# A scan and a gated feed-forward layer in fp32: weight exponents moved to ScalarE, norm scales folded into the weights, two gate tiles ahead of the norm, and every block written as a list of small steps

## The chip, the cores and the metric

The kernel runs on one core of one Trainium2 chip. The metric is device time in microseconds (us); the figure shown for a kernel is the median of its runs. The core's engines are TensorE (PE for its matmuls, PEld for its weight loads), VectorE (DVE), ScalarE (ACT), GpSimd (POOL) and SyncE (SP), which here issues nearly all DMAs. Each engine executes its own list of instructions in order, and semaphores make one engine wait for another.

## The reference

A chunked state-space scan over 4 batches x 8 heads x 768 tokens feeds a gated feed-forward layer over 3072 tokens x 256 channels.

```python
for c in range(nc):                       # chunks of 32 tokens
    cum = np.cumsum(la, axis=-1)          # la = log(clip(a))
    L = np.exp(cum[..., :, None] - cum[..., None, :]) * causal
    M = np.einsum('bhin,bhjn->bhij', Cc, Bc) * L
    y_intra = np.einsum('bhij,bhjd->bhid', M, xc)
    y_inter = np.einsum('bhin,bhnd->bhid', Cc, state) * np.exp(cum)[..., None]
    state = decay_full * state + sum(Bx)
x = y.transpose(0, 2, 1, 3).reshape(B * S, H * D)
xn = x / np.sqrt(np.mean(x * x, -1) + 1e-6) * rms_g
g = xn @ w_gate                           # 256 x 1536
out = (g / (1 + np.exp(-g)) * (xn @ w_val)) @ w_out   # 1536 x 256
```

The three weight matrices come in float64; the other inputs are float32.

## The kernel before, in words

The scan works in chunks of 128 tokens, two at a time: a *pair* `p` of 256 tokens. There are 12 pairs. Two pairs make a *block* of 512 tokens, of which there are six (0 to 5), and the feed-forward layer works block by block. While PE runs block `b`'s feed-forward products, the scan of block `b + 1` is threaded between them.

**Weights.** Float64 weights arrive as pairs of 32-bit words in 20 pieces (`fetch`): four small ones of 2 x 128 columns, ten of 2 x 256 for gate and value, six of the output matrix. `begin` and `finish` turn a piece into fp32. DVE masks the exponent bits (L157), ACT turns them into a power of two in two passes (L160, L161), DVE builds the mantissa (L163, L166), ors the sign into the power (L172) and multiplies (L174). At most nine pieces are fetched ahead; the next fetch is issued by a `begin`.

**Scan of a pair.** `pad` spreads C into a zeroed tile (GpSimd, in pair 0 half of it DVE, L384), `scale` multiplies B and C by decays, `turn` transposes them on PE (L405) and copies them out of PSUM (L407), `products` form C times B (L428) and multiply by the decay matrix `L` (L436, L447), `states` form the new state (L459 to L476), `outputs` sum up (L494, L503), square on ACT (L519), add on GpSimd (L520) and copy out (L521). For the first four pairs the decay matrices come from PE (`mask`, `sums`) and an exponential; later ones are broadcast by a DMA from a table in DRAM (`spread`, L367), reduced by a subtraction on DVE (L373), exponentiated (L376) and masked on GpSimd (L377).

**Norm.** `norm_sums` makes the mean square on PE (L531) and the inverse root on GpSimd (L536); `norm_apply` spreads it by a PE transpose (L544) and multiplies on DVE by the norm and by `rms_g` (L550).

**Feed-forward.** In block 0, 12 tiles of gate and value (L567, 128 x 512 each), a silu (L575), a product (L580), then the projection (L688). Blocks 1 to 5 use a seven-product scheme over 2 x 2 blocks of the operands, which replaces one of eight products by additions: for each pair of tiles `j` (six of them) products 1 to 7 (L619) into two PSUM banks, with copies on ACT (L624), sums `c` (L629), silus (L634) and hidden products (L638) between them; then the projection in the same scheme (L724), whose operands are made by in-place differences of the hidden tiles on DVE (L709, L710, L756, L762). `combine_w`, `combine_x`, `combine_wo` make the operands' combinations.

**Order.** The tile framework is told to keep the order of the program text, so each engine's list is the order in which the Python calls stand. In block 0 that is a hand-written sequence with lists of conversions per tile (`plan`) and of scan steps per tile (`scan_steps`); in blocks 1 to 5 it is the loop in `gates_and_values` and the sequence in `projection`, with scan steps hung into it (`todo`, `extras`).

## Time and profile before

| | |
|---|---|
| Time, median of 3 runs | 448.68 us (448.5 to 453.81) |
| The profiled execution, its own time | 445.7 us |
| Its span | 444.0 us |
| PE / DVE / ACT busy | 425.4 / 321.1 / 197.7 us |
| Granted TensorE clock | 1.0 |

A row of a timeline gives the start, the time from the first start to the last end of a run of like instructions, the engine, the line, the operation, output and input tiles, shape and count; the bracket is the engine's idle time ahead of it and who ended it. A matmul of fp32 shows as two records, so x16 are eight matmuls. A row of the grouped views gives, behind the bar, busy time, mean nanoseconds of one, and the idle time ahead with its releaser. Since PE's ends are modelled and overlap the next start, its standing time is better read from starts.

### The profile page before, as it was taken

Reading aid. Unit: us, or ns where it says so; the run is one execution under the profiler, and the core shown is the slowest. Engines: PE = TensorE matmul, PEld = TensorE weight load, DVE = VectorE, ACT = ScalarE, POOL = GpSimd, SP = SyncE. Lnnn points to the kernel's source line nnn. Section 1 sums busy time; section 2 is a strip of 40 time slices with the busy share of each in tenths; the row PEclk is TensorE's granted clock in tenths of the full one; section 3 lists DMA queues with packets and bytes.
Section 4 is the critical chain, followed back from the end, with each engine's and each line's share of the span. In section 5 each row is a group of like instructions: output and inputs, shape, how many; then the busy total and the mean of one; then the engine's idle time right before and its main releaser. Section 6 shows DMA issues by size and latency. Waiting matters only on the chain.

```text
span 444.0 us, 7771 instructions
## 1 busy us (share of the span) xinstructions
PE 425.4 (96%) x3066; PEld 340.6 (77%) x3066; DVE 321.1 (72%) x669; ACT 197.7 (45%) x370; POOL 51.7 (12%) x73
## 2 busy tenths in 40 slices
PE   7988999898999998999998999998999999999996
PEld 4654454386777788987788987788987789988896
DVE  5769997589887988466858566868557855467661
ACT  3467553435644353446453446453345440155510
POOL 4030000013200005100005200004200001000000
PEclk9999999999999999999999999999999999999999
DMA  9884443760433120432320341330100000100001
GB/s 137 182 208 138 153 119 103 228 86 0 83 37 81 38 97 3 73 47 47 73 96 2 67 52 26 94 96 1 48 1 1 0 1 1 47 3 0 1 1 47
DMA packets 86564, 27.99 MB, mean 63 GB/s; under 512 B 76000, under 2 KB 80352, under 8 KB 86528
## 3 DMA queue, kind: packets, MB, share of 16 engines
q1 hardware_dynamic: 82368, 27.24, 26.7%
q10 hardware_dynamic: 4160, 0.26, 0.8%
q8 instruction: 24, 0.39, 0.3%
q14 instruction: 12, 0.10, 0.1%
HBM read 24.22 MB, written 3.28 MB: 62 GB/s over the span
## 4 chain that ended last, share of the span: by engine, by line
PE 82%; DVE 11%; SPq 2%; DMA 2%; issue 1%; ACT 0%; POOL 0%; DVEq 0%
PE gate L619 24%; PE o L724 21%; PE val L619 17%; PE gate L567 6%; PE g L428 4%; PE y L503 3%; PE tp L405 2%; SPq L108 2%; PE y L494 2%; DMA xr<-in_x_dram 1%; DVE e L172 1%; PE o L688 1%; DVE L L373 1%; DVE s L756 1%; DVE m L166 1%; DVE sw L597 1%
## 5 line engine op out<-in xcount | busy, mean ns | idle before, releaser
L629 DVE TENSOR_TENSOR c<-val,p 128x512 f32<-128x512 f32 x90 | 60.7, 687 | 44.6 <-PE val L619 36.8
L624 ACT COPY p<-gate 128x512 f32<-128x512 f32 x90 | 52.8, 587 | 51.9 <-PE gate L619 51.7
L619 PE MATMUL gate<-tx,sw 128*128 128x256 f32 x240 | 63.7, 388 | 0.7 <-ACT p L624 0.7
L634 ACT ACTIVATE c<-c 128x256 f32<-128x256 f32 x90 | 37.8, 420 | 46.4 <-DVE c L629 46.4
L619 PEld LDWEIGHTS gate<-tx,sw 128*128 128x128 f32 x240 | 42.7, 190 | 9.9 <-issue 3.3
L638 DVE TENSOR_TENSOR h<-c 128x256 f32<-128x256 f32 x90 | 37.7, 419 | 12.6 <-ACT c L634 12.6
L567 PE MATMUL gate<-xn,wgv 128*128 128x512 f32 x96 | 43.7, 599 | 1.2 <-DVE wgv L174 1.2
L724 PE MATMUL o<-two,s 128*128 128x128 f32 x240 | 30.4, 278 | 4.1 <-DVE s L756 4.1
L520 POOL TENSOR_TENSOR sq<-sq 128x256 f32<-128x256 f32 x12 | 8.9, 744 | 218.3 <-ACT sq L519 218.3
L567 PEld LDWEIGHTS gate<-xn,wgv 128*128 128x128 f32 x96 | 17.3, 190 | 20.4 <-issue 17.4
L377 POOL TENSOR_SCALAR_AFFINE_SELECT L<-L 128x1024 f32<-128x1024 f32 x16 | 24.7, 1552 | 68.1 <-ACT L L376 68.1
L724 PEld LDWEIGHTS o<-two,s 128*128 128x128 f32 x240 | 28.2, 192 | 5.1 <-ACT v L735 2.4
L619 PE MATMUL val<-xn,sw 128*128 128x256 f32 x120 | 31.7, 386 | 0.0
L619 PE MATMUL val<-tx,sw 128*128 128x256 f32 x120 | 31.3, 383 | 0.1
L619 PE MATMUL gate<-tx,wgv 128*128 128x256 f32 x120 | 30.9, 380 | 0.0
L619 PE MATMUL gate<-xn,wgv 128*128 128x256 f32 x120 | 30.8, 379 | 0.0
L619 PE MATMUL val<-xn,wgv 128*128 128x256 f32 x120 | 30.8, 379 | 0.0
L724 PE MATMUL o<-wo,h 128*128 128x128 f32 x240 | 30.0, 275 | 0.0
L724 PEld LDWEIGHTS o<-wo,h 128*128 128x128 f32 x240 | 29.2, 192 | 0.5
L376 ACT ACTIVATE L<-L 128x1024 f32<-128x1024 f32 x16 | 16.9, 1057 | 28.4 <-DVE L L373 28.1
L724 PE MATMUL o<-two,h 128*128 128x128 f32 x240 | 27.6, 275 | 0.0
L724 PEld LDWEIGHTS o<-two,h 128*128 128x128 f32 x240 | 27.2, 192 | 0.0
(147 smaller groups left out, 706.8 us busy)
## 6 DMA issues: line engine op xcount, KB each, us to landing
L<-rowd SPq DMA_DIRECT2D x16, 512.0 KB, 4.7
xr<-in_x_dram SPq DMA_DIRECT2D x24, 128.0 KB, 3.1
wr<-in_moe_w_out_dram SPq DMA_DIRECT2D x6, 512.0 KB, 3.4
wr<-in_moe_w_gate_dram SPq DMA_DIRECT2D x5, 512.0 KB, 5.9
wr<-in_moe_w_val_dram SPq DMA_DIRECT2D x5, 512.0 KB, 4.9
out_dram<-ob SPq DMA_DIRECT2D x10, 256.0 KB, 2.1
br<-in_B_dram SPq DMA_DIRECT2D x22, 64.0 KB, 2.9
cr<-in_C_dram SPq DMA_DIRECT2D x22, 64.0 KB, 3.0
```

What stands on the lines that cost most here:

```text
L376: nc.scalar.activation(out=L, in_=L, func=AF.Exp)
L377: nc.gpsimd.affine_select(out=L, in_=L, pattern=[[0, NH], [1, P]], compare_op=ALU.is_ge, fill=0.0, base=0, channel_multiplier=-1)
L428: nc.tensor.matmul(out=g[:, 256 * i:256 * i + 256], lhsT=T[r, i, 0], rhs=T[r, i, 1:3].rearrange("p t m -> p (t m)"), start=(i == 0), stop= ...
L503: nc.tensor.matmul(out=y[o:o + 32, h // 4, i * P:(i + 1) * P], lhsT=s["x"][:, i, h], rhs=Ls[p][:, i, h], start=opens, stop=True, tile_posi ...
L520: nc.gpsimd.tensor_tensor(out=sqs[blk][:, tk], in0=sq2[:, 0], in1=sq2[:, 1], op=ALU.add)
L567: nc.tensor.matmul(out=gv[:, k], lhsT=w[:, t, fs], rhs=xns[blk][:, t], start=(t == 0), stop=(t == 1))
L619: nc.tensor.matmul(out=dst[:, half[w]], lhsT=lhsT, rhs=rhs[k], start=(opens and w == 0), stop=True, skip_group_check=True)
L624: nc.scalar.copy(out=t, in_=src)
L629: nc.vector.tensor_tensor(out=c, in0=b, in1=a, op=ALU.add)
L634: nc.scalar.activation(out=u, in_=c[:, half[0]], func=AF.Silu)
L638: nc.vector.tensor_tensor(out=hidden_tile(blk, j)[:, f, k], in0=u, in1=c[:, half[1]], op=ALU.mult)
L724: nc.tensor.matmul(out=o[:, t * P:(t + 1) * P], lhsT=lhsT[:, t], rhs=rhs, start=(opens and j == 0 and t == 0), stop=True, skip_group_check ...
```

## The change

The computation is the same. Five things differ:

- **Powers of two.** ACT reads the top 16 bits of each double (sign, exponent, four bits of mantissa) and makes the signed power of two as a bf16 in three passes: a relu with a 16-bit integer result and two parametric relus. DVE's exponent mask and its sign step are gone; DVE keeps the mantissa (two steps) and the last product, which now issues the next fetch. ACT loads its function table four times more often in all.
- **Norm scales.** `rms_g` times 2^-20 is the scalar of the gate and value weights' last product, which is therefore made in two halves of 128 input channels; the norm's application is one product of 128 x 1024 in place of two of 128 x 512.
- **Two tiles ahead of the norm.** Gate and value tiles 0 and 1 of block 0 are multiplied from the scan's output itself, each in two halves of 256 tokens (`early`); DVE multiplies the result by the inverse root, once for the gate and once for the value (`norm`), and ACT's silu then works in place.
- **Small steps.** Functions are split where one engine hands over to another (`sums_of_logs` and `three_parts`, `turn` and `turned`, `products` and `decayed`, `states`, `outputs`, `norm_sums`, `gates_and_values`, `projection`), and all that follows the set-up is two lists of such steps: one for the head and block 0, one that serves blocks 1 to 5 (a step that has no block to work for is skipped). Block 0's PSUM slots are given out by a small bookkeeping (`take`, `leave`).
- **Engines.** The copies of the scan's output of pairs 0 and 1 move from ACT to DVE.

```diff
+    def power(k):
+        words16, (lo, hi), dst, shape, is_o = fetched[k]
+        n = shape[1] * shape[2]
+        e = cvt.tile([P, n], FP32, tag="e", name="e")
...
+        nc.scalar.activation(out=k16, in_=words16, func=AF.Relu, scale=1.0 / 16, bias=kinks[:, 0:1])
+        nc.scalar.activation(out=g, in_=k16, func=AF.Prelu, scale=-1.0, bias=kinks[:, 1:2],
+                             alpha=2.0 ** -20)
+        nc.scalar.activation(out=b16, in_=g, func=AF.Prelu, scale=-2.0 ** 27, bias=kinks[:, 2:3],
+                             alpha=2.0 ** -20)
...
+    def weight(k):
+        words16, (lo, hi), dst, shape, is_o = fetched[k]
+        e, f = parts.pop((k, "e")), parts.pop((k, "f"))
+        if is_o:
+            nc.vector.scalar_tensor_tensor(out=dst, in0=f, scalar=2.0 ** -20, in1=e,
+                                           op0=ALU.mult, op1=ALU.mult)
+        else:
+            for t in range(2):
+                nc.vector.scalar_tensor_tensor(out=dst[:, t], in0=f[:, t], scalar=g20[:, t:t + 1],
+                                               in1=e[:, t], op0=ALU.mult, op1=ALU.mult)
+        fetch()
...
-    def norm_apply(blk, ks):
...
+    def norm_apply(blk):
+        rb = ps["rb"].rearrange("p k m -> p (k m)")
+        xns[blk] = nrm.tile([P, 2, TB], FP32, tag="xn", name="xn", bufs=1)
+        nc.vector.tensor_tensor(out=xns[blk], in0=yts[blk],
+                                in1=rb.unsqueeze(1).to_broadcast([P, 2, TB]), op=ALU.mult)
...
+    def products_early(f, s, gv):
+        ps["gv", f] = gv
+        fs = slice(f * P, (f + 1) * P)
+        tk = slice(s * 256, s * 256 + 256)
+        for k, w in enumerate((wg, wv)):
+            for t in range(2):
+                nc.tensor.matmul(out=gv[:, k, tk], lhsT=w[:, t, fs], rhs=yts[0][:, t, tk],
+                                 start=(s == 0 and t == 0), stop=(t == 1),
+                                 skip_group_check=True)
...
+    def normed(f):
+        gv = ps.pop(("gv", f))
+        us[f] = ffn.tile([P, TB], FP32, tag="u", name="u", bufs=2)
+        for k, dst in enumerate((us[f], of_block_0(f))):
+            nc.vector.tensor_tensor(out=dst, in0=gv[:, k], in1=ps["r"], op=ALU.mult)
...
+    order = """
+        pad.0 mask.0.1 r.0 d mask.0.0 c parts.0 turn.0.0 dx turn.0.1 T.0.0 cx sums.0.0 pad.1 exp.0.0
...
```

In the list of blocks 1 to 5, `P.k.j` is gate product `k` of tile pair `j`, `O.k.j` the same of the projection, `sub.g` the subtraction for chunk `g` of the block after next, `ms`, `rs`, `rb`, `xn` the norm of the next block. How this moves instructions shows at three places.

**DVE, first weights and the norm of block 0.** `e`, `m` and `wgv` are the exponent, the mantissa and the finished gate and value weights; `me` is the mean square, `yt` the scan's output. Before:

```order
L157 TENSOR_SCALAR e<-wr 128x256
L163 TENSOR_SCALAR m<-wr 128x256
L166 SCALAR_TENSOR_TENSOR m<-wr,m 128x256
L534 TENSOR_SCALAR me<-ms 128x4
L172 SCALAR_TENSOR_TENSOR e<-wr,e 128x256
L174 SCALAR_TENSOR_TENSOR wgv<-m,e 128x2x128
```

Now:

```order
L489 TENSOR_TENSOR L<-g,L 128x2x2x256 x3
L524 TENSOR_TENSOR A<-A_ps,tmask 128x128
L534 SCALAR_TENSOR_TENSOR S<-S,fcol,A 128x64 x2
L190 SCALAR_TENSOR_TENSOR wgv<-m,g_190,e 128x128 x2
L587 COPY yt<-y 128x2x256
```

The first weights are finished right behind the scan of pair 1, ahead of the norm's mean square, and no exponent step of DVE stands among them.

**DVE, projection of block 0.** `wo` are the output weights, `tok` the sums that are subtracted from the broadcast decay tile `L`. Before:

```order
L157 TENSOR_SCALAR e<-wr 128x512
L163 TENSOR_SCALAR m<-wr 128x512
L166 SCALAR_TENSOR_TENSOR m<-wr,m 128x512
L172 SCALAR_TENSOR_TENSOR e<-wr,e 128x512
L174 SCALAR_TENSOR_TENSOR wo<-m,e 128x512
L373 TENSOR_TENSOR L<-L,tok 128x1024
```

Now:

```order
L600 TENSOR_SCALAR me<-ms 128x4
L175 TENSOR_SCALAR m<-wr 128x512
L178 SCALAR_TENSOR_TENSOR m<-wr,m 128x512
L186 SCALAR_TENSOR_TENSOR wo<-m,e 128x512
L408 TENSOR_TENSOR L<-L,tok 128x1024 x3
L186 SCALAR_TENSOR_TENSOR wo<-m,e 128x512
L618 TENSOR_TENSOR xn<-yt,rb 128x1024
```

Three steps make a piece in place of five, and the last pieces are done between the subtractions, before the norm of block 1.

**PE, end of the gate products of blocks 1 to 5.** `ms` and `rb` are the norm's sums and its spread root; `s` and `two` are the combined operands of the projection. Before:

```order
L724 MATMUL o<-two,s 128x128 x2
L531 MATMUL ms<-mean_194,sq 128x1 x4
L724 MATMUL o<-two,s 128x128 x12
L724 MATMUL o<-wo,h 128x128 x12
L544 MATMUL rb<-ident,rs 128x128 x4
```

Now:

```order
L795 MATMUL o<-two,s 128x128 x2
L595 MATMUL ms<-mean_195,sq 128x1 x4
L716 MATMUL val<-xn,sw 128x256 x2
L716 MATMUL gate<-tx,wgv 128x256 x2
L795 MATMUL o<-two,s 128x128 x4
L795 MATMUL o<-wo,h 128x128 x6
L795 MATMUL o<-two,s 128x128 x2
L608 MATMUL rb<-ident,rs 128x128 x4
```

The sums of the norm stand ahead of the last gate products, and groups of the projection's first and fifth product lie between them and the spread root.

More of the change, by code (lines that the diff above doesn't have):

```diff
@@ L800 @@
-    turn(0, 1, nc.vector.tensor_copy, 3)
-    sums([(1, 0, ey)])
-    decay(1, 0, ey)
-    products(0, 0)
-    pad(1, nc.gpsimd)
-    turn(1, 0, nc.scalar.copy, 3)
-    turn(1, 1, nc.scalar.copy, 3)
-    ez = masked()
-    sums([(0, 1, ez)])
-    decay(0, 1, ez)
-    scale(0)
-    products(1, 0)
-    full_ps = bank("full_ps", (P, NC, BH))
-    nc.tensor.matmul(out=full_ps.rearrange("p c h -> p (c h)"), lhsT=ones, rhs=laf,
-                     start=True, stop=True)
-    nc.scalar.activation(out=full, in_=full_ps, func=AF.Exp)
@@ L944 @@
+    """
+    for step in order.split():
+        kind, *numbers = step.split(".")
+        kinds[kind](*map(int, numbers))
     nc.scalar.preload_act_table(AF.Silu)
```

722 lines of the change are left out of this document (340 added, 382 removed).

## The prediction

> **What bounds the kernel now.** I read the page's first and fourth part, then the stretches by stage, then the timeline of TensorE (PE) alone for the places where it stands still. First the page:
>
> ```profile
> PE 425.4 (96%) x3066; PEld 340.6 (77%) x3066; DVE 321.1 (72%) x669; ACT 197.7 (45%) x370; POOL 51.7 (12%) x73
> ...
> PE 82%; DVE 11%; SPq 2%; DMA 2%; issue 1%; ACT 0%; POOL 0%; DVEq 0%
> ```
>
> PE is the bound, and VectorE (DVE) is what it waits for. The stretches run from the last scan output of block 0 to its third gate tile, the other gates of block 0, its projection, block 1, block 3. Columns are the stretch, its length, busy time (instructions) of PE, PEld, DVE, ACT and POOL, granted clock, DMA share, GB/s.
>
> ```profile
> 25.01:40.18 15.17, 13.09 (x84) 6.66 (x81) 11.77 (x29) 13.45 (x21) 3.37 (x6) 1.00 0.58 130
> 40.18:88.69 48.51, 46.23 (x242) 21.85 (x242) 40.95 (x76) 23.73 (x40) 1.45 (x2) 1.00 0.51 158
> 88.69:113.86 25.17, 22.96 (x109) 19.38 (x110) 23.56 (x38) 11.66 (x14) 5.80 (x5) 1.00 0.31 38
> 113.86:181.00 67.14, 64.96 (x498) 54.81 (x497) 58.74 (x124) 30.54 (x63) 10.71 (x11) 1.00 0.25 56
> ...
> 248.00:315.00 67.00, 65.87 (x508) 56.76 (x507) 46.92 (x97) 30.85 (x59) 9.95 (x11) 1.00 0.27 56
> ```
>
> From 40 to 114 us DVE is busy 64.5 of 73.7 us: the weights' conversion is there. In block 3 it has 20 us to spare, and PE is nearly full. The clock is full throughout. So a gain can only be PE's standing time, which I take from starts: what lies between two starts less the dense time of the first group.
>
> ```profile
> 10.99 0.33 PE L405 MATMUL tp<-ident,cp 128*128 128x128 f32 x1 [0.89 <-DVE cp L384]
> ...
> 23.24 0.45 PE L494 MATMUL y<-T,S 32*64 32x128 f32 x8 [0.74 <-ACT T L415]
> ...
> 29.13 0.65 PE L544 MATMUL rb<-ident,rs 128*128 128x128 f32 x4 [0.87 <-POOL rs L536]
> ...
> 31.34 7.19 PE L567 MATMUL gate<-xn,wgv 128*128 128x512 f32 x16
> 38.37 0.27 PE L405 MATMUL tp<-ident,br 128*128 128x128 f32 x1
> ...
> 40.18 3.67 PE L567 MATMUL gate<-xn,wgv 128*128 128x512 f32 x8 [1.21 <-DVE wgv L174]
> ...
> 53.51 1.13 PE L428 MATMUL g<-T 32*128 32x256 f32 x8 [0.87 <-DVE h L580]
> ```
>
> ```profile
> 83.58 3.70 PE L567 MATMUL gate<-xn,wgv 128*128 128x512 f32 x8
> 88.69 1.99 PE L688 MATMUL o<-wo,h 128*128 128x256 f32 x8 [1.41 <-DVE h L580]
> ...
> 101.17 3.72 PE L688 MATMUL o<-wo,h 128*128 128x256 f32 x16 [0.52 <-DVE wo L174]
> 105.93 3.72 PE L688 MATMUL o<-wo,h 128*128 128x256 f32 x16 [1.04 <-DVE wo L174]
> 110.30 3.72 PE L688 MATMUL o<-wo,h 128*128 128x256 f32 x16 [0.65 <-DVE wo L174]
> 113.86 1.03 PE L619 MATMUL gate<-xn,wgv 128*128 128x256 f32 x4
> 114.72 1.03 PE L619 MATMUL val<-xn,wgv 128*128 128x256 f32 x4
> 116.42 1.13 PE L619 MATMUL gate<-tx,sw 128*128 128x256 f32 x4 [0.67 <-ACT p L624]
> ```
>
> Sixteen gate matmuls take 38.37 - 31.34 = 7.03 us, so eight take 3.52: after 83.58 the next could start at 87.10 and starts at 88.69, 1.6 us late. Sixteen of L688 take 113.86 - 110.30 = 3.56, so the steps of 4.76 and 4.37 lose 1.20 and 0.81. A bracket is smaller than such a loss by about 0.2 us, since PE's modelled end overhangs the next start. A gate product of block 1 takes 114.72 - 113.86 = 0.86. Counted so, the places ahead of 40.18 lose 1.1, 0.9, 1.0 and 1.4; those from there to 113.86 lose 1.0, 1.6, 0.7, 1.2 and 0.8. Block 1 opens with 0.8. Within a block there is one place, here in block 3:
>
> ```profile
> 301.55 0.95 PE L531 MATMUL ms<-mean,sq 128*128 128x1 f32 x8
> 303.18 0.68 PE L724 MATMUL o<-two,s 128*128 128x128 f32 x4 [0.68 <-DVE s L756]
> 304.31 1.94 PE L724 MATMUL o<-two,s 128*128 128x128 f32 x15 [0.45 <-DVE s L756]
> ```
>
> PE waits for DVE's in-place differences (L756), 0.9 and then 0.6 us.
>
> **The change part by part.** (a) Conversion. The rows of one 512-column weight piece, among the DVE groups with shapes kept apart, with three that later steps use:
>
> ```profile
> L629 DVE TENSOR_TENSOR c<-val,p 128x512 f32<-128x512 f32 x90 | 60.7, 687 | 44.6 <-PE val L619 36.8 <-ACT p L624 7.5
> L638 DVE TENSOR_TENSOR h<-c 128x256 f32<-128x256 f32 x90 | 37.7, 419 | 12.6 <-ACT c L634 12.6
> ...
> L172 DVE SCALAR_TENSOR_TENSOR e<-wr,e 128x512 int32<-128x512 int32 x16 | 11.9, 744 | 2.1 <-ACT e L161 2.1
> L166 DVE SCALAR_TENSOR_TENSOR m<-wr,m 128x512 f32<-128x512 uint32 x16 | 11.1, 695 | 0.5
> ...
> L580 DVE TENSOR_TENSOR h<-u,gate 128x512 f32<-128x512 f32 x12 | 8.2, 682 | 4.7 <-ACT u L575 4.7
> ...
> L157 DVE TENSOR_SCALAR e<-wr 128x512 int32<-128x512 int32 x16 | 7.0, 439 | 0.1
> L174 DVE SCALAR_TENSOR_TENSOR wgv<-m,e 128x512 f32<-128x512 f32 x10 | 6.9, 692 | 0.3
> L163 DVE TENSOR_SCALAR m<-wr 128x512 int32<-128x512 int32 x16 | 6.7, 422 | 0.0
> ...
> L174 DVE SCALAR_TENSOR_TENSOR wgv<-m,e 128x256 f32<-128x256 f32 x4 | 1.7, 425 | 0.1
> ```
>
> And on ACT:
>
> ```profile
> L624 ACT COPY p<-gate 128x512 f32<-128x512 f32 x90 | 52.8, 587 | 51.9 <-PE gate L619 51.7
> ...
> L161 ACT ACTIVATE e<-e,einf 128x512 int32<-128x512 f32 x16 | 11.6, 722 | 0.5
> ```
>
> DVE loses L157 and L172, 0.44 + 0.74 = 1.18 us a piece, and pays 2 x 0.425 - 0.692 = 0.16 where a gate or value piece is now multiplied in two halves. With 10 such pieces, 6 of the output weights and four small ones at about half, that is 10 x 1.02 + 6 x 1.18 + 4 x 0.5 = 19 us less on DVE, 18 of them between 25 and 114. Given back there are two tiles normed by hand (four 512-wide products like L580's, 0.68 each) and two copies of the scan's output (about 0.6 each, below L580's): 4 us. DVE then has about 62 us of work in the 89 us that were, where 76.3 us are busy now. Of this nothing is gained by itself; it lets DVE be in time.
>
> Scalar (ACT) does three passes in place of two. No row shows the parametric relu or a 16-bit result; nearest is L161, 0.72 us. Below it lies L624's 0.59, also 512 wide; above it twice the row if 16-bit words went at half speed. I take 0.72: a piece costs 2.2 us, 20 pieces add 18 x 0.72 = 13 us (small ones at half), and ACT has 23.73 + 11.66 = 35.4 busy in 73.7 us: covered. At twice the row, 48 large passes add 35 us, more than the cover leaves.
>
> The Trainium skill's "ScalarE: Activation LUTs", section "What ACT_TABLE_LOAD costs", gives 280 ns plus 0.833 ns an element for any function with a bias by pointer; worked out, an estimate of 0.706 us for 512, near the 0.722 row. It says so of fp32 and bf16 alone; by it the rival with dear passes would have no chance at all.
>
> (b) Head, to gate tile 2. The order puts the transposes before the decay sums, both block-0 halves first, and lets two gate tiles run on the un-normed output. The losses of 1.1 (pad copy on DVE, which now comes before the log sums), 0.9 and 1.0 go; PE has the row sums, transposes and pair-2 sums to do meanwhile. For the 1.4 (weights late behind DVE) a new wait comes: the second early tile needs its fourth small piece, whose step on DVE stands behind the root of the norm, two scalings and one mantissa. From the copy of the second output on (24.5) DVE has a mantissa and a weight step of a small piece, four steps of log-sum parts, another mantissa (to about 28.2), waits for PE's `ms` (29.2), then two scalings (0.8), a large mantissa (L163 and L166, 1.1) and the small weight step (0.5): 31.7. PE has two early halves (1.8 each), masks, `ms`, two decay sums and, after GpSimd's root, the turned norm: 31.1. So 4.4 less 1.0 for that and small ones: **3.4**, of which I keep 2.9, since the start still hangs on the loads.
>
> (c) Gates of block 0: 1.0 + 1.6. The `g` products find their bank earlier, and the projection no longer starts behind the last gate: its first group and a scan output stand between gate tile 10 and the next groups. **2.4**.
>
> (d) Projection: 0.7 + 1.2 + 0.8 = 2.7. DVE's work between gate 10 and the last group is 20 us (three weight steps, four subtractions at 1.2, two combinations of four at 0.42, the norm) against 22 us of PE. **2.3**.
>
> (e) Block 1 opens without waiting for ACT's copies, since the four exponentials end before the last group, and its first transposes and products of two tiles lie between: **1.0**.
>
> (f) Norm and differences in blocks 1 to 4: 0.9 + 0.6, in block 4 0.9 alone, 5.4 in all. Two gate products and five output groups now stand between `ms` and the first `6` product. DVE has to do, from the last gate product on, one subtraction (1.22), the last sum `c` (L629, 0.69), six hidden products (L638, 0.42), three sums of the same width: about 5.5 us with what has begun, then 1.3 to the difference of tile 0; PE has seven output products of 0.45 (four records each; 15 take 1.94 with the overhang), the turned norm at 0.5 and six more products before it needs it: 6.4 us. So about 0.4 stays there and 0.4 where the `7` products need DVE again: 0.8 a block, 3 in all. **2.4**.
>
> The sum is 2.9 + 2.4 + 2.3 + 1.0 + 2.4 = 11.0 us; less 0.5 for the two split tiles and the extra switches of tile shape, **10.5**. Table loads rise by four, which ACT's idle 36 us a block hide. The profiled execution took 445.7 us (span 444.0), so 435.2; the median shown is 448.68, so 438.2.
>
> One more row bears on (f): GpSimd's mask of the decays (L377) runs beside DVE.
>
> ```profile
> L373 DVE TENSOR_TENSOR L<-L,tok x16: 1210/1218/2104, 101.0 to 313.9; 128x1024 f32<-128x1024 f32 x16
> ...
> L377 POOL TENSOR_SCALAR_AFFINE_SELECT L<-L x16: 1087/1290/2941, 103.4 to 316.2; 128x1024 f32<-128x1024 f32 x16
> ...
> DMA to landing us min/median/max: 3.4/4.7/7.0
> ```
>
> The third row is the landing time of the broadcasts that fill this tile. A subtraction of 1.22 us takes up to 2.10 then. In the new order two masks fall on the differences; if DVE runs at half speed beside each, it loses 0.6 to a mask, and (f) falls to 2.4 - 3.6 and the time is 441.8. The Trainium skill's "GPSIMD Engine Reference", section "1. Specifications", speaks against the change here: GpSimd shares its SBUF interface with DVE and contends with DVE instructions of two SBUF inputs, which the differences are. That the stretched subtraction has two such inputs agrees with it; that most of the sixteen stand at 1218 ns shows that it does not always bite.
>
> **The rivals.** First, **PE's waits come back elsewhere**: the two engines are packed against each other, and a wait on DVE delays ACT and PE in turn. For it speaks that DVE has by my count 17 us of work in the 20 us of a block's output products, against it its 20 idle us a block. If (f) gives nothing, and half of (c) and (d) returns: 10.5 - 2.4 - 2.4 = 5.7, hence 443 us.
>
> Second, the slower side: **DVE stands for a load in the middle of a block**. The subtraction for the first of the next pairs moved from the projection to between the gate products, and the broadcast that feeds it can only start when the block's first scan output has left the buffer. On the SP queue the next pair's loads stand behind that broadcast, which no one needs within 10 us. Behind the subtraction on DVE stand the sums and hidden products that free the bank for PE's fifth tile. Between that output and the subtraction PE runs five gate products and the `g` products (L428, 1.1): 5 x 0.86 + 1.1, so DVE gets there 5.3 us after that output. At a landing of 4.7 there is no wait, at 7.0 it is 1.8 us in three blocks, 5.4; from 8.7 us on the gain is eaten, and at the 9.2 us that a weight load took in the crowded first 40 us (the row below, of the raw weight tile in that window) it is 3 x 4.0 = 12, hence 450 us.
>
> ```profile
> DMA to landing us min/median/max: 3.6/5.1/9.2
> ```
>
> Against it: DMA share is 0.27 in block 3.
>
> Third, ACT's passes at twice the row: of the 40 us that ACT is idle between 25 and 114, 13 go to the third pass and 7 to the shorter stretch, and 35 us on the 20 that are left cost 15, hence 453 us.
>
> **How the numbers follow.** My forecast 0.55; waits come back 0.35; the load 0.06; dear passes 0.04. Its own range is 433 to 441. The range 431 to 446 takes in 443, contended masks (441.8) and, below, a block phase without any wait (5.4 in place of 2.4, and 1.4 more at the head: 433.8, with 3 us for the scatter of the median). Two per cent, about what a measurement can tell from no change, is 9.0 us: 439.7. The forecast lies 1.5 us inside. Faster: three quarters of the forecast and a third of the first rival, 0.53. Slower by over 2% (457.7): only the far ends of the last two and what I have not seen, 0.04. Within: 0.43.
>
> **What would show it.** DVE's conversion rows fall by about 19 us and ACT's three rows stand at 0.7 us; the first group of block 1 (113.86 now) starts at 106 to 108; no wait of PE for `wo` over 0.3; blocks 2 and 3 take 66.0 to 66.5 in place of 67.0. It is wrong if a PE wait of over 1 us stands in every block, if the 16-bit passes exceed 1 us, or if DVE idles at the mid-block subtraction.

## The result, and the profile after

The changed kernel takes **426.73 us** (median of 4 runs, 425.22 to 426.94), the kernel before 448.59 (448.01 to 453.81) beside it: a ratio of 0.9489, with a 95% interval of 0.9423 to 0.9554. The forecast was 438.2 with a range of 431 to 446: the sign was right, and the gain of 21.9 us was twice the 10.5 foreseen. Executions in which the clock was down for long are left out of the comparisons below; the one of 453.81 is still in here, and without it the ratio is 0.951.

The first and the fourth part of the page of the changed kernel:

```profile
PE 418.5 (98%) x3082; PEld 348.3 (82%) x3082; DVE 305.5 (72%) x645; ACT 209.6 (49%) x393; POOL 50.7 (12%) x73
...
PE 91%; DVE 5%; issue 1%; DMA 1%; POOL 0%; DVEq 0%; POOLq 0%
```

VectorE's (DVE's) share of the chain that ended last fell from 11 to 5%, although DVE is as busy as before in share (72%). It is in time more often; it does not do much less.

The prediction's stretch for block 3 began and ended inside blocks. Here are stretches from the start of one stage to that of the next, in the kernel before and then in the changed one: gate tile 2 to the first product of block 1, and block 3. The columns are those of the stretches in the prediction.

```profile
40.18:113.86 73.68, 69.19 (x351) 41.24 (x352) 64.52 (x113) 35.40 (x54) 7.25 (x7) 1.00 0.44 117
...
250.54:317.80 67.26, 66.13 (x510) 57.02 (x509) 47.18 (x96) 30.99 (x59) 9.95 (x13) 1.00 0.27 56
```

```profile
39.21:105.16 65.95, 65.95 (x341) 41.00 (x341) 54.50 (x102) 49.56 (x71) 9.16 (x11) 1.00 0.43 114
...
236.37:301.70 65.33, 64.95 (x510) 57.45 (x509) 47.75 (x96) 30.94 (x61) 9.73 (x12) 1.00 0.26 57
```

| stage, from starts in the traces | before | after | gain | predicted |
|---|---|---|---|---|
| to gate tile 2 | 40.18 | 39.21 | 1.0 | 2.9 (b) |
| gate tile 2 to block 1 | 73.68 | 65.95 | 7.7 | 4.7 (c, d) |
| blocks 1 to 4 (69.3, 67.4, 67.3, 66.9; now 65.8, 65.4, 65.3, 64.8) | 270.86 | 261.29 | 9.6 | 3.4 (e, f) |
| block 5 and what lies around | 60.98 | 60.49 | 0.5 | 0 |
| shape switches and split tiles | | | in the rows above | -0.5 |
| profiled execution | 445.7 | 426.94 | 18.8 | 10.5 |

From gate tile 2 to block 1 none of the five waits that the prediction listed is left between the starts of TensorE (PE); by its modelled ends it is busy 65.95 of 65.95 us. What is left stands at two places. One is in the head (PE's timeline):

```profile
29.95 0.65 PE L608 MATMUL rb<-ident,rs 128*128 128x128 f32 x4 [0.85 <-POOL rs L602]
30.43 3.16 PE L647 MATMUL gate<-yt,wgv 128*128 128x256 f32 x8
...
34.72 1.89 PE L647 MATMUL gate<-yt,wgv 128*128 128x256 f32 x8
```

PE waits for the norm's root, and then the same eight matmuls take 3.16 us at 30.43 and 1.89 at 34.72. The stretches of that place say why; the column behind the five engines is the granted clock:

```profile
28.00:29.90 1.90, 1.09 (x21) 0.66 (x20) 1.83 (x7) 1.74 (x3) 1.15 (x1) 1.00 0.56 53
...
31.50:32.50 1.00, 1.00 (x3) 0.77 (x3) 1.00 (x2) 0.00 (x0) 0.99 (x2) 0.50 1.21 123
...
34.70:36.40 1.70, 1.70 (x10) 1.50 (x9) 0.00 (x0) 1.45 (x3) 0.00 (x0) 1.00 0.63 230
```

Behind the wait the clock is 0.50. By the starts of the matmuls that lasts from 30.87 to 34.24, 3.4 us (the trace's record of the clock has 0.50 for 3.41 us from 30.89 on), and costs half of it, 1.7 us. The other place is in the projection of blocks 1 to 3, here block 3, first on PE, then on DVE and GpSimd (POOL):

```profile
294.81 0.61 PE L795 MATMUL o<-two,h 128*128 128x128 f32 x4
295.80 2.05 PE L795 MATMUL o<-two,h 128*128 128x128 f32 x16 [0.38 <-DVE h L773]
```

```profile
291.22 2.54 DVE L773 TENSOR_TENSOR h<-h 128x256 f32<-128x256 f32 x2
293.68 1.30 DVE L408 TENSOR_TENSOR L<-L,tok 128x1024 f32<-128x1024 f32 x1
294.91 0.84 DVE L773 TENSOR_TENSOR h<-h 128x256 f32<-128x256 f32 x2
...
291.16 2.32 POOL L415 TENSOR_SCALAR_AFFINE_SELECT L<-L 128x1024 f32<-128x1024 f32 x2 [6.55 <-ACT L L414]
```

A group of four takes 0.45, so of the 0.99 us between those two starts 0.55 are lost. Two differences that take 0.84 together at 294.91 take 2.54 beside the two masks that begin at 291.16.

The subtraction on DVE that was moved, and ScalarE's (ACT's) three passes, among the groups with shapes kept apart:

```profile
L408 DVE TENSOR_TENSOR L<-L,tok 128x1024 f32<-128x1024 f32 x16 | 20.5, 1284 | 1.2 <-DMA L<-rowd 1.2
...
L165 ACT ACTIVATE e<-wr,kinks 128x512 int16<-128x512 int16 x16 | 12.2, 763 | 0.5 <-DVE wgv L190 0.5
L166 ACT ACTIVATE e<-e,kinks 128x512 f32<-128x512 int16 x16 | 11.6, 722 | 0.5
L168 ACT ACTIVATE e<-e,kinks 128x512 int16<-128x512 f32 x16 | 11.6, 722 | 0.5
```

The passes stand at the 0.72 us foreseen, the first slightly above it.

### The profile page after: what moved, and what is told of

Read it like the earlier page. It is cut to its first block, busy times and chain, and to the rows that moved or that the text cites. A ratio compares the mean times of both kernels' runs of the same rounds, so it can differ in the third digit from the quotient of the medians.

```text
span 425.2 us, 7817 instructions
## 1 busy us (share of the span) xinstructions
PE 418.5 (98%) x3082; PEld 348.3 (82%) x3082; DVE 305.5 (72%) x645; ACT 209.6 (49%) x393; POOL 50.7 (12%) x73
## 4 chain that ended last, share of the span: by engine, by line
PE 91%; DVE 5%; issue 1%; DMA 1%; POOL 0%; DVEq 0%; POOLq 0%
PE gate L716 25%; PE val L716 19%; PE o L795 18%; PE gate L637 8%; PE o L748 5%; PE g L479 4%; PE tp L452 3%; PE y L561 2%; DVE h L773 2%; PE y L552 2%; PE gate L647 1%; DMA cr<-in_C_dram 1%; PE e L373 1%; PE ms L595 1%; DVE xn L618 1%
## 5 line engine op out<-in xcount | busy, mean ns | idle before, releaser
L716 PE MATMUL gate<-tx,sw 128*128 128x256 f32 x240 | 60.8, 379 | 0.0
L716 PEld LDWEIGHTS gate<-tx,sw 128*128 128x128 f32 x240 | 45.6, 190 | 6.2
L737 ACT ACTIVATE c<-c 128x256 f32<-128x256 f32 x90 | 34.8, 416 | 5.1 <-DVE c L728 5.1
L637 PE MATMUL gate<-xn,wgv 128*128 128x512 f32 x80 | 36.1, 598 | 0.0
L795 PE MATMUL o<-two,h 128*128 128x128 f32 x240 | 32.5, 277 | 1.1 <-DVE h L773 1.1
L795 PE MATMUL o<-wo,h 128*128 128x128 f32 x240 | 33.3, 275 | 0.0
L795 PE MATMUL o<-two,s 128*128 128x128 f32 x240 | 33.3, 275 | 0.0
L807 ACT COPY v<-o 128x256 f32<-128x256 f32 x15 | 5.6, 372 | 52.0 <-PE o L795 52.0
L737 ACT ACTIVATE u<-gate 128x256 f32<-128x256 f32 x30 | 11.4, 380 | 37.9 <-PE gate L716 37.9
L637 PEld LDWEIGHTS gate<-xn,wgv 128*128 128x128 f32 x80 | 14.7, 190 | 16.5 <-issue 13.9
```

What stands on the lines that cost most here:

```text
L637: nc.tensor.matmul(out=gv[:, k], lhsT=w[:, t, fs], rhs=xns[0][:, t], start=(t == 0), stop=(t == 1))
L716: nc.tensor.matmul(out=dst[:, half[w]], lhsT=lhsT, rhs=rhs, start=(k in (1, 2, 5) and w == 0), stop=True, skip_group_check=True)
L737: nc.scalar.activation(out=u, in_=src[:, half[0]], func=AF.Silu)
L795: nc.tensor.matmul(out=o[:, t * P:(t + 1) * P], lhsT=lhsT[:, t], rhs=rhs, start=(k in (1, 2, 4, 5) and j == 0 and t == 0), stop=True, skip ...
```

## The experiments

The theory after the traces: the gain is PE's standing time in three parts, long waits, many short steps at shape switches, and the half clock behind waits. The rival: the gain comes from relieving DVE, wherever the steps stand.

**The list of blocks 1 to 5, put back.** The kernel is the changed one with the second list in the sequence before:

```diff
-        turn.0.0 scale.1 P.1.0 cw.2 turn.0.1 cw.3 take.1.0 cw.4 P.1.1 T.0.0 T.0.1 take.1.1 P.2.0
+        P.1.0 take.1.0 P.2.0 C.11.0 cw.2 P.6.0 take.6.0 silu.11.0 hid.11.0 P.5.0 turn.0.0 T.0.0
...
```

> The changed kernel with the list of blocks 1 to 5 put back into the sequence of the kernel before (the same 257 steps); conversion, head and block 0 as changed. By the sum of the prediction (terms e and f, 1.0 + 2.4) it should be 3.4 us slower than the changed kernel. By the starts in the two traces (blocks 1 to 4 became 3.6, 1.9, 1.9 and 2.2 us shorter, block 5 0.5) it should be about 10 us slower, with blocks 2 and 3 back at 67.3 us. If the gain of the blocks came from the head or from the weights' arithmetic and not from the list, it stays within 1.5 us of the changed kernel.

435.98 us (435.07 to 438.54), ratio to before 0.9747 (0.9705 to 0.979): 9.3 over the changed kernel. Blocks 1 to 4 take 68.2, 69.0, 68.8 and 66.9 us, and block 5, to the end of the span, 59.2. Blocks 4 and 5 are those of the kernel before; blocks 2 and 3 are 1.6 longer, since the half clock came behind the waits for the differences there (0.57 granted in the second row, starts 223.3 to 227.1):

```profile
218.00:223.00 5.00, 4.14 (x36) 3.89 (x35) 3.84 (x7) 2.51 (x3) 1.38 (x2) 1.00 0.00 0
223.20:227.00 3.80, 3.73 (x19) 3.73 (x20) 3.80 (x8) 1.20 (x2) 1.04 (x2) 0.57 0.02 4
```

Without that half clock (1.6 in each of two blocks) the old list costs 8.9 us in blocks 1 to 5, of the 10.0 that they gained: the list carries nearly all of the blocks' gain, and not 3.4. The other 1.1 is in block 1, which behind the changed block 0 takes 68.2 us with the old list and not 69.3. That the medians differ by 9.3 is in part chance: the profiled execution reached block 1 at 101.16, 4.0 us ahead of the changed kernel's, for reasons that stand under the filled waits below.

**Half of that list each.** First everything behind the last gate product as before:

```diff
         silu.11.5 silu.22.4 P.5.5
-        C.12.4 O.1.0 O.1.1 take.7.5 hid.11.3 C.22.5 O.5.0 ms P.3.5 P.4.5
+        s3.0 s3.1 hid.11.3 load.1 s3.2 s.3 s3.3 hid.22.4 C.12.4 hid.11.5
+        spread.3 silu.12.4 hid.12.4 s.4 s3.4 take.7.5 C.22.5 O.1.0 O.1.1 O.1.2 P.4.5 silu.22.5
...
```

> The changed kernel; in the list of blocks 1 to 5 everything behind the last gate product stands as in the kernel before. If the two waits at the differences are the blocks' loss, they come back (0.93 behind the sums of squares, since VectorE stands for them with the differences queued behind; 0.62 beside GpSimd's mask; 0.55 goes): 1.0 us a block in blocks 1 to 3 and 0.9 in block 4, about 4 us in all over the changed kernel. If the shape switches among the gates are the loss, nothing comes back here.

437.37 us (436.39 to 438.21). Behind the sums of squares the 0.93 us are back in all four blocks. But the 0.62 is not there, and 1.22 and 0.54 us stand in all five blocks at the last gate products, which now run behind output products for which they don't fit. The cut made waits of its own, so only the 0.93 is read from it.

Then everything up to the gates' last sum `C.22.5` as before, with the first differences that stand among the gates there:

```diff
-        turn.0.0 scale.1 P.1.0 cw.2 turn.0.1 cw.3 take.1.0 cw.4 P.1.1 T.0.0 T.0.1 take.1.1 P.2.0
+        P.1.0 take.1.0 P.2.0 C.11.0 cw.2 P.6.0 take.6.0 silu.11.0 hid.11.0 P.5.0 turn.0.0 T.0.0
...
+        silu.12.4 hid.12.4 s.4 s3.4 take.7.5 C.22.5 sub.0 table O.1.0 O.1.1 O.5.0 ms P.3.5 P.4.5
...
```

> The changed kernel; in the list of blocks 1 to 5 everything up to the last gate product stands as in the kernel before, the rest as changed. By the small steps between starts (0.03 to 0.25 us each: 3.70 a block before, 2.80 now) it is 0.9 us a block slower than the changed kernel, some 4 us with the opening of block 1. If the blocks' gain is at the differences alone, it is within 1 us of the changed kernel.

429.32 us (426.92 to 430.24), 2.6 over the changed kernel; by starts blocks 1 to 5 are 4.0 longer, and the profiled execution met no half clock in its head. Block 3:

```profile
233.75:299.56 65.81, 65.81 (x510) 56.86 (x509) 47.96 (x96) 31.90 (x61) 9.35 (x11) 1.00 0.26 57
```

Blocks 2 and 3 take 65.9 and 65.8 against 65.4 and 65.3, without any wait over 0.25 us, so also without the 0.55 (five of the six differences are done among the gates here). The old gate order costs 0.5 + 0.55 = 1.0 us in each of these two; 0.9 was expected. In part it is visits to other tile shapes, PE in the kernel before and in the changed one:

```profile
265.90 1.03 PE L619 MATMUL gate<-tx,sw 128*128 128x256 f32 x4
266.84 1.13 PE L619 MATMUL val<-xn,sw 128*128 128x256 f32 x4
...
268.77 0.32 PE L459 MATMUL A_ps<-xr,Bd 128*32 128x64 f32 x8
...
271.24 1.03 PE L619 MATMUL val<-xn,wgv 128*128 128x256 f32 x4
272.11 1.03 PE L619 MATMUL gate<-tx,wgv 128*128 128x256 f32 x4
273.06 0.45 PE L494 MATMUL y<-T,S 32*64 32x128 f32 x8
```

```profile
252.87 0.32 PE L512 MATMUL A_ps<-xr,Bd 128*32 128x64 f32 x8
253.12 0.45 PE L552 MATMUL y<-T,S 32*64 32x128 f32 x8
...
254.88 1.13 PE L716 MATMUL val<-xn,sw 128*128 128x256 f32 x4
255.85 1.03 PE L716 MATMUL gate<-xn,wgv 128*128 128x256 f32 x4
```

A gate product in front of another takes 272.11 - 271.24 = 0.87 us. In front of the small tiles of the scan it takes 0.95 (272.11 to 273.06), and the one behind them 0.97 (254.88 to 255.85): a visit to another tile shape costs 0.08 + 0.10. Before, the additions and the outputs of a pair were two visits; now they are one, so block 3 has four visits for six, some 0.4 us. The steps of 0.03 to 0.25 us between starts sum to 3.70 us in block 3 before, 2.79 now. The other half of that difference is no visit: before, a gate product took 0.94 and not 0.87 (265.90 to 266.84) with full tiles on both sides, and the next one 0.97 again. Block 3 has three such places before and none now; what makes them was not tried.

**One instruction moved.** In the kernel before, the addition that reads the sums of squares is put behind the six second differences, and nothing else is touched (`norm_roots` holds the addition and GpSimd's root):

```diff
+        sums_[blk] = ms
+        if blk < 2:
+            norm_roots(blk, ks)
...
             extras[1].append((norm_sums, blk + 1, range(NT)))
+            extras[2].append((norm_roots, blk + 1, range(NT)))
```

> The kernel before with one VectorE instruction a block moved: the addition that reads the sums of squares stands behind the six second differences, not ahead of them (with GpSimd's root behind it). If TensorE's 0.93 us wait comes from VectorE standing 1.09 us for the sums with the differences queued behind, it is gone in blocks 1 to 4: 3 to 4 us faster, and the half clock with it. If the differences are late by themselves, nothing changes.

**441.69 us** (441.47 to 441.94), ratio 0.9856 (0.9836 to 0.9877). DVE and POOL in the kernel before:

```profile
300.23 1.22 DVE L373 TENSOR_TENSOR L<-L,tok 128x1024 f32<-128x1024 f32 x1
302.54 0.16 DVE L534 TENSOR_SCALAR me<-ms 128x4 f32<-128x4 f32 x1 [1.09 <-PE ms L531]
302.62 2.98 DVE L756 TENSOR_TENSOR s<-s,h 128x256 f32<-128x256 f32 x6
...
302.66 1.32 POOL L377 TENSOR_SCALAR_AFFINE_SELECT L<-L 128x1024 f32<-128x1024 f32 x1 [10.16 <-ACT L L376]
```

DVE, and then PE, in this one:

```profile
298.23 1.22 DVE L373 TENSOR_TENSOR L<-L,tok 128x1024 f32<-128x1024 f32 x1
299.36 2.10 DVE L765 TENSOR_TENSOR s<-s,h 128x256 f32<-128x256 f32 x6
301.38 0.15 DVE L543 TENSOR_SCALAR me<-ms 128x4 f32<-128x4 f32 x1
...
299.55 0.95 PE L531 MATMUL ms<-mean,sq 128*128 128x1 f32 x8
300.85 2.94 PE L733 MATMUL o<-two,s 128*128 128x128 f32 x24 [0.35 <-ACT v L744]
```

Before, DVE stood 1.09 us for PE's sums with the differences queued behind, and PE then stood for the differences: each waited for the other through the order of DVE's queue. With the addition behind them the six differences begin 1.1 us after the subtraction did (not 2.4) and take 2.10 us and not 2.98; PE is left with 0.6 us for one of ACT's copies. Blocks 1 to 4 are 1.0, 1.0, 1.0 and 0.8 us shorter, 3.8 in all. The other 2.8 of the 6.6 us by medians are about what the clock makes: it is 1.00 in four of five runs.

**No mask.** The changed kernel without the mask in `exponential`:

```diff
         nc.scalar.activation(out=L, in_=L, func=AF.Exp)
-        nc.gpsimd.affine_select(out=L, in_=L, pattern=[[0, NH], [1, P]], compare_op=ALU.is_ge,
-                                fill=0.0, base=0, channel_multiplier=-1)
```

> The changed kernel without GpSimd's masks of the broadcast decays, so the part of each decay above the diagonal is left unmasked. If a mask holds the VectorE operation that starts beside it, the differences' longest falls from 1310 ns to about 420 and TensorE's wait of 0.55 us at the products 7 of blocks 1 to 3 is gone: about 1.6 us faster. If the wait comes from the amount of VectorE work, it stays.

424.76 us (421.55 to 424.9). Blocks 1 to 3 take 65.2, 64.8 and 64.7, which is 0.6 less each, and the 0.55 us wait is gone. The differences with the shortest, median and longest ns, first in the changed kernel and then here (two line numbers less, since a statement is gone):

```profile
L773 DVE TENSOR_TENSOR h<-h x30: 409/418/1310, 155.1 to 412.0; 128x256 f32<-128x256 f32 x30
```

```profile
L771 DVE TENSOR_TENSOR h<-h x30: 412/418/508, 155.0 to 409.9; 128x256 f32<-128x256 f32 x30
```

So the mask, and not the amount of DVE work, made that wait.

**The conversion alone.** The kernel before with the three ACT passes and the norm scales in the weights, and no order touched. The bodies of `power` and `weight` stand in `begin` and `finish`, and the norm is one product without the gain vector. In the first form the scaling of the gain vector was the first DVE instruction that needed a load:

```diff
+    g20 = const.tile([P, 2], FP32, name="g20")
+    nc.vector.tensor_scalar(out=g20, in0=gcol, scalar1=2.0 ** -20, scalar2=None, op0=ALU.mult)
+    kinks = const.tile([P, 3], FP32, name="kinks")
```

> The kernel before with only the conversion changed: three ScalarE passes for the power of two, the norm scale in the weights, no step order touched. If the order is what pays, only the waits that a weight step ended can go (1.4 ahead of gate tile 2, 2.7 in the projection, part of the 2.6 among the gates): 2 to 5 us faster than the kernel before, and blocks 2 and 3 stay at 67.3 us. If relief of VectorE is the main thing, the first product of block 1 comes 8 us earlier, near 105. If the longer ScalarE passes hurt where no order makes room for them, it is not faster at all.

455.83 us (454.24 to 459.32), slower than before, ratio 1.0185 (1.0124 to 1.0247). The row tells it:

```profile
13.24 0.17 DVE L262 TENSOR_SCALAR g<-gcol 128x2 f32<-128x2 f32 x1 [9.57 <-DMA gcol<-in_moe_rms_g_dram]
```

An instruction of 0.17 us held all of DVE for 9.57, and behind that wait PE had half the clock from 9.72 to 26.79. With it behind the first scan outputs:

```diff
     convert("bb")
+    nc.vector.tensor_scalar(out=g20, in0=gcol, scalar1=2.0 ** -20, scalar2=None, op0=ALU.mult)
     ex, ey = masked(), masked()
```

> The kernel before with only the conversion changed, and the scaling of the gain vector put behind the first scan outputs of block 0 (in the run before it stood first on VectorE and waited 9.6 us for its load). As there: 2 to 5 us faster than the kernel before if relief of VectorE removes the waits that a weight step ended; first product of block 1 near 105 if relief is the main thing; no gain if the three ScalarE passes stand in the way of the copies that TensorE needs. Blocks 2 and 3 stay at 67.3 us in each case.

445.54 us (444.88 to 446.27), ratio 0.9944 (0.9927 to 0.9961): 2.5 us faster. The waits of the projection for `wo` are gone (22.2 us for 25.2); the 0.93 and 0.62 us at the differences stand as before.

**The order alone.** The changed kernel with the old power of two:

```diff
-        nc.scalar.activation(out=k16, in_=words16, func=AF.Relu, scale=1.0 / 16, bias=kinks[:, 0:1])
...
+        nc.vector.tensor_scalar(out=ei, in0=hi, scalar1=0x7FF00000, scalar2=None,
+                                op0=ALU.bitwise_and)
+        nc.scalar.activation(out=ef, in_=ei, func=AF.Relu, scale=-8.0, bias=etop)
+        nc.scalar.activation(out=ei, in_=ef, func=AF.Relu, scale=-1.0, bias=einf)
...
+        nc.vector.scalar_tensor_tensor(out=ei, in0=hi, scalar=-2 ** 31, in1=ei,
+                                       op0=ALU.bitwise_and, op1=ALU.bitwise_or)
```

> The changed kernel with the old arithmetic of the power of two: mask and sign step on VectorE, two ScalarE passes (two of the power steps stand one place later in the list, since VectorE now waits for their buffer). If the order alone carries the head and block 0, it is within 1.5 us of the changed kernel. If the order needs the 18 us that VectorE was relieved of, VectorE is full from 25 to 105 us (65.8 busy now, of 80, so about 84 wanted) and the first product of block 1 comes 4 to 8 us later, with blocks 2 to 5 as in the changed kernel.

438.58 us (436.99 to 438.96), ratio 0.978 (0.9756 to 0.9804). From gate tile 2 to block 1, here and with the conversion alone:

```profile
40.89:114.31 73.42, 68.59 (x341) 41.36 (x341) 68.63 (x126) 39.95 (x57) 10.20 (x11) 0.98 0.41 109
```

```profile
41.32:111.53 70.21, 68.63 (x351) 41.26 (x351) 52.22 (x90) 48.31 (x72) 8.72 (x8) 1.00 0.45 120
```

That stretch is 73.7 us before, 73.4 with the order alone (71.7 without 1.7 us of half clock that fell there), 70.2 with the conversion alone and 65.95 with both. The order gains 2.0 there, with DVE busy 68.6 of 73.4 us; the relief gains 3.5 in an order that can't use it; together they gain 7.7, some 2 more than the two alone. Block 1 takes 66.6 (65.8 in the changed kernel), and from block 2 on the blocks are the changed kernel's.

**Without the early tiles.** Tiles 0 and 1 behind the norm:

```diff
-        early.0.0 wt.2 early.0.1
+        wt.2
...
-        wt.3 rb early.1.0 mask.3.1 turn.2.0 early.1.1 rc turn.2.1
+        wt.3 rb mask.3.1 turn.2.0 turn.2.1
...
-        norm.1 xn.0 pad.3 exp.3.0 sums.3.1 wt.5 man.6 g.2.0 exp.3.1
+        xn.0 gate.0 pad.3 exp.3.0 sums.3.1 wt.5 man.6 silu.0 gate.1 exp.3.1
```

> The changed kernel without the two gate tiles ahead of the norm: tiles 0 and 1 follow the norm as the others do. If those tiles cover the norm, the third gate tile (39.2 us now) starts 2 to 4 us later and the whole is as much slower. If the late weight pieces set the pace there, it starts within 0.7 us of where it does, and the time stays.

431.24 to 436.84 us, ratio 0.9692 (0.9624 to 0.9759). Gate tile 2 starts at 43.25 and not 39.21: that is 4.0 us later, and 3.8 are left at block 1 (108.98 for 105.16). The two heads met the clock differently (half clock for 6.8 us from 24.24 on here, for 3.4 in the changed kernel), so the 4.0 is not the early tiles' alone.

**Filling the waits.** Matmuls of constants where PE stands, in the kernel before (`fill`) and in the changed kernel (`rb.10`), into a bank that no one reads or that the turned norm overwrites:

```diff
-            extras[1].append((norm_sums, blk + 1, range(NT)))
+            extras[1] += [(norm_sums, blk + 1, range(NT)), (fill, 9)]
...
-        man.4 wt.3 rb early.1.0
+        man.4 wt.3 rb.10 early.1.0
```

> The kernel before with nine 256-column bfloat16 matmuls of constants behind the sums of squares of blocks 2 to 5, into a bank nobody reads: about 1 us of TensorE work where it stands 0.93 us for the differences. Left as it is: every other instruction. If the low use of TensorE around that wait is what brings the half clock (granted clock 0.991 in 8 of the 13 runs of the kernel before in the last comparison), the clock is 0.996 or 1.00 in most runs and the time falls from 447.9 to about 446, although work was added. If the clock drops for another reason, it stays at 0.991 and the time at 447.9 to 448.5.

445.93 us (445.32 to 446.51) beside 448.26, ratio 0.9949 (0.9929 to 0.9969), with a clock of 0.994 to 1.00 in six runs; the kernel before has 0.991 or 0.992 in seven of eleven beside it (and in six of the thirteen that the expectation speaks of, not eight). Blocks 2 and 3 are not shorter (67.38, 67.27).

> The changed kernel with ten such matmuls in the head, ahead of the turning of the norm, where TensorE stands 1.0 us for GpSimd's root. If the low use there brings the half clock behind it (30.9 to 34.2 us in the changed kernel's trace, 0.996 over the run), the clock is 1.00 and the time 1.5 to 2 us below the changed kernel's. If not, the time is the changed kernel's or a little more.

423.65 us (423.59 to 425.41), 3.1 under the changed kernel, with 0.999 or 1.00 in all six runs where the changed kernel has 0.996 in all four. PE's timeline:

```profile
28.35 0.60 PE L611 MATMUL rb<-ident,rs 128*128 128x128 f32 x4
28.78 1.89 PE L650 MATMUL gate<-yt,wgv 128*128 128x256 f32 x8
...
35.87 0.70 PE L640 MATMUL gate<-xn,wgv 128*128 128x512 f32 x1
```

The early tile takes 1.89 and not 3.16. Work was added to both kernels, and both became faster: the half clock comes from PE's low use, and goes with it. From the first early tile to gate tile 2 it is 14.6 us (35.87 - 21.27) where it was 16.1. `old_gates_new_tail` has the head of the changed kernel, and its profiled execution met no half clock there: 14.4. So the half clock cost 1.7 us, and the filling gains 1.5 of the 3.1.

The rest is no effect of the filling. The first early tile starts at 21.27 and not 23.11, and in `old_gates_new_tail`, without any filling, at 21.26. The rows of one decay sum tell why, in the changed kernel and in the filled one:

```profile
6.49 0.85 PE L338 MATMUL d_ps<-la,upto 128*128 128x192 f32 x2
```

```profile
6.01 0.49 PE L338 MATMUL d_ps<-la,upto 128*128 128x192 f32 x2
```

PE's first matmuls run at half speed: the next sum starts 0.64 us later in the changed kernel and 0.33 in the filled one. The traces' record of the clock begins at 10.41 us in the one and at 5.23 in the other, and only from there on is PE at full speed; ahead of it the stretches print 1.00, since nothing is on record. Times of one kernel that stand 1.6 to 1.7 us apart at the same granted clock (425.22 and 426.8 at 0.996, 421.68 and 423.36 at 1.00) fit this start, but no kernel has the traces of two executions to show it.

**Both places mended.** The changed kernel with `ms.0` behind the first half of the first early tile, the masks and decay sums of pair 2 behind the turned norm, and four differences in DVE's idle time ahead of the masks:

```diff
-        early.0.0 wt.2 early.0.1 mask.2.1 ms.0 parts.1 sums.2.0 pad.2 sums.2.1 pow.3 man.3 pow.4
-        rs scale.2 exp.2.0 exp.2.1 man.4 wt.3 rb early.1.0 mask.3.1 turn.2.0 early.1.1 rc
+        early.0.0 ms.0 wt.2 rs early.0.1 man.3 wt.3 pow.4 rb parts.1 early.1.0 rc sums.2.0
+        exp.2.0 norm.0 early.1.1 pow.5 mask.2.1 man.4 sums.2.1 scale.2 exp.2.1
...
-        s2.1 Otake.1 s2.5
+        s2.1 s3.1 s3.3 s3.4 s3.5 Otake.1 s2.5
```

> The changed kernel with two places of its lists altered. In the head the norm's sums stand behind the first half of the first early tile, so that the root is ready while TensorE has the second early tile to do; the in-place differences s3.1, s3.3, s3.4, s3.5 stand in VectorE's 1.5 us of idle time ahead of s2.5 and so ahead of GpSimd's masks. If the 1.0 us wait for the root and the stretch of half clock behind it (3.4 us, 1.7 lost) hang together, gate tile 2 starts 2 to 3 us earlier and the granted clock stays at 1.00 there; if the clock drops on its own, it drops there as well. If the mask beside a difference makes the 0.55 us wait of the products 7, that wait is gone in blocks 1 to 3: 1.6 us. Together 3 to 5 us faster than the changed kernel; if the loads set the head, 1.6.

**423.36 us** (421.68 to 423.37), ratio 0.9443 (0.9409 to 0.9478): 3.4 under the changed kernel by medians, with runs that don't overlap, and a clock of 1.00 in all four. PE in its head, and block 3:

```profile
24.76 1.02 PE L595 MATMUL ms<-mean,sq 128*128 128x1 f32 x8
25.64 1.97 PE L647 MATMUL gate<-yt,wgv 128*128 128x256 f32 x8
27.45 0.60 PE L608 MATMUL rb<-ident,rs 128*128 128x128 f32 x4
27.89 1.89 PE L647 MATMUL gate<-yt,wgv 128*128 128x256 f32 x8
```

```profile
233.42:298.09 64.67, 64.67 (x510) 57.35 (x509) 47.77 (x96) 30.94 (x61) 9.74 (x12) 1.00 0.26 58
```

Gate tile 2 starts at 37.49, 1.7 earlier; from the start of the first early tile it is 14.6 us, as in the filled kernel. So what is gained there is the half clock: the 1.0 us at the root is gone as well, but PE is no further, since it loses as much in short steps behind. Blocks 1 to 3 gain 0.6 each, as without masks.

## Why the prediction was wrong in size

**Terms (e) and (f) failed most: 3.4 for 10.1.** The failing step is (f): it counted DVE's work ahead of the differences and not what DVE waited for. (e) was near: the long waits of block 1 ahead of its differences (0.8, 0.3 and 0.4) are gone, 1.5 for 1.0. In (f) two things were missed. First, it costed the waits at the differences by counting DVE's work between the last gate product and the differences, and so kept 0.8 us a block. It did not ask what stood in front of them in DVE's queue. That was an instruction that waited for PE itself (sum_later). With that knot undone, 0.55 us a block stays in blocks 1 to 3 and none in block 4; of 5.6 us of waits 4.0 went. Second, it counted only steps over some 0.3 us and booked the scan's shape switches as a loss of 0.5 together with the split tiles. The short steps fell by 0.8 to 1.0 us in each of four blocks, 3.6 in all; in block 3 nearly half of it is fewer visits (old_gates_new_tail).

**Terms (c) and (d): 4.7 for 7.7.** The listed waits (5.3) went without remainder, short steps gave 1.1 more, and about 1.3 us are scan matmuls that now run in the head (351 matmuls in that stretch before, 341 now). That there would be no wait for `wo` over 0.3 us held; the first product of block 1 came at 105.16, just ahead of the 106 to 108 forecast. The reason given, DVE in time, is shown: with the old power of two the stretch is back at 73.4, or 71.7 at full clock.

**Term (b): 2.9 for 1.0.** A new wait of 1.0 was foreseen, and it came, but for the root and not for the fourth small piece. What was not foreseen is the half clock behind it, 1.7 us: without it 2.7 would have been gained, and that with the matmuls that moved here. Another 1.8 us went to the slow first matmuls of the profiled execution. In `old_gates_new_tail`, with the same head and neither of the two, gate tile 2 starts at 35.65, 4.5 us ahead of the kernel before. So the order of the head was worth more than the term said, and the clock hid it.

**The step from the profile to the median failed too.** The text said "the clock is full throughout", which held for the profiled execution, and then carried its 3.0 us of distance to the median over to the forecast. That distance was the half clock of the other executions: the kernel before takes 445.7 to 445.9 us at 1.00 and 447.9 to 448.8 at 0.991 or 0.992. No kept trace of that kernel has the half clock, but in those of kernels with the same waits it stands right behind them (from 223.76 and 292.03 on in `old_blocks`, 302.30 in `new_powers_2`), and filling them brought the clock to 0.994 or more (before_filled). The change removes these waits, so that loss went with them. The changed kernel's median lies at its profiled time. The terms together: 6.7 + 3.0 - 1.9 from (e), (f), (c), (d) and (b), 0.5 for the switches, 3.2 from the median are 11.5 us, the distance between 438.2 and 426.7.

**What held.** The conversion takes 36.8 us of DVE for 55.9, the 19 foreseen. ACT's passes are at 0.72 to 0.76, so the rival with dear passes was out. DVE stood once, 1.2 us, for a broadcast, so the load in the middle of a block did not bite. Contended masks were weighed at 3.6 us and are there: 0.55 us of PE's time in each of three blocks. The Trainium skill's "GPSIMD Engine Reference", section "1. Specifications", was cited for it, and the traces bear it out in kind: beside a mask a difference takes 1.31 us for 0.42, while none of the four operations of the changed kernel that read PSUM and started there was longer. But the kernel before had the same loss (1.31 for one of its second differences), so it was not new with the change.

Two readings of the prediction were wrong without moving the forecast. That most of the sixteen subtractions take 1218 ns does not show that a mask beside them sometimes does no harm: in the trace only the one of 2104 ns, at 110.17, lay beside a mask. And in the rival of the load, 5 x 0.86 + 1.1 is 5.4 and not 5.3, while its waits of 1.8 and 4.0 us go by 5.2.

## What to carry to other kernels

Where two engines wait for each other, look at what stands at the head of the late engine's queue before counting its work: one addition, moved by six places, was worth 1.4% of this kernel. Sum the short steps between starts as well as the listed waits, and count visits to other tile shapes. If the profiled execution is faster than the median of the runs, compare the granted clocks before carrying the distance over: here a wait of 1 us on TensorE cost 1.7 more behind it. Compare the first matmuls of two traces as well, since a head that starts at half speed shows in no granted clock.

## What the runs showed of the hardware

- Behind a wait of about 1 us amid small matmuls, TensorE's granted clock was 0.50 for 3.41 us (from 30.89 on in the changed kernel, from 223.76 and 292.03 on in `old_blocks`). Filling the wait with matmuls of constants removed it in the head of the changed kernel, and raised the clock of the kernel before from 0.991 or 0.992 to 0.994 or more. In all fourteen kept traces the clock is 1.00 or 0.50, and each change lies a whole multiple of 3.41 us behind the first. The Trainium skill's "TensorE: Matmul & The Clock Gate", section "Part 1: The HAM clock gate (the "warmup" mystery)", has the clock halved after an idle window of about 3.4 us that runs freely; the length agrees, and a window that runs freely would account for the same program meeting it in one execution and not in the next. Here far less than 3.4 us of standing sufficed.
- TensorE's first matmuls ran at half speed, until 3.8 to 10.4 us into the span, and the record of the clock has nothing ahead of that. Between 5.2 and 10.4 us that moved the first early tile by 1.8 us.
- A DVE operation with both inputs in SBUF that started beside GpSimd's mask was in most cases held for most of the mask: 0.42 became 1.31 us. A mask that started beside a run of such operations was held in its place: 2.94 us for 1.29, while five differences of the kernel before kept their 0.41 (from 308.13 on).
- A visit to matmuls of another tile shape cost 0.08 us going in and 0.10 coming back to gate products. Steps of the same size also stood at three places of block 3 before where no other shape was near.
